# The first loads of a gated pair of linear-attention blocks: one queue in order of need, four chunks of x turned by TensorE

## The chip, the cores and the metric

The kernel runs on one core of a Trainium2 chip. The metric is the time of one execution on the device in microseconds (us), lower is better; a comparison takes the median of several runs. Traces are taken by the hardware profiler on one execution; times in them count from the span's start.

## The reference

Two linear-attention blocks A and B read the same `x` (2048 rows, 640 columns, bf16) and have their own weights. Their outputs are mixed by a gate computed per row from `x` and `gate_w`.

```python
def block(x, wqkv, wo):                      # 32 heads of 20
    q, k, v = split(x @ wqkv)                # each [head, 2048, 20]
    phi = lambda t: where(t > 0, t + 1, exp(t)) + 1e-6
    pq, pk = phi(q), phi(k)
    kv = einsum("bhsd,bhse->bhde", pk, v)
    z = einsum("bhsd->bhd", pk)
    num = einsum("bhqd,bhde->bhqe", pq, kv)
    den = einsum("bhqd,bhd->bhq", pq, z)[..., None] + 1e-6
    return merge_heads(num / den) @ wo

g = sigmoid((x * gate_w).sum(-1, keepdims=True))
out = g * block(x, A_wqkv, A_wo) + (1 - g) * block(x, B_wqkv, B_wo)
```

## The kernel before

All the matmuls need `x` twice: natural (`xn`, 16 chunks of 128 rows) and turned (`xT`, 640 columns on the partitions as 5 slices of 128, by 2048 rows). The k part of block A is made chunk by chunk: ten matmuls for a chunk of 128 rows (5 slices `c` times two halves `hf` of 320 columns), accumulated in a PSUM tile of two banks. The second half is one column wider (321): that column of `wkA` holds `gate_w`, so that the gate's logits fall out of the same matmul. `phi` then takes the PSUM tile through an exponential on ScalarE (ACT), and a `tensor_scalar` and a `scalar_tensor_tensor` on VectorE (DVE) into `pk`. The q part (`q_block`, `q_single`) multiplies slices of `wqA` with 512 rows of `xT`, and goes through the same `phi`. After k and q of A come the products G = x^T pk (partly by Strassen's scheme), normalisers, k and q of B, G of B, small products with `wv` and `wo`, and at the end the output products; nothing of that is touched by the change.

PSUM is used as four slots of two banks each (`ps(name, slot)`, tags ps0 to ps3); outside the hand-ordered parts `turn` hands them out in rotation, and after `k_first` it is set to 2.

The order at the start comes from the program for what lies in `tc.manual_schedule()`, which keeps each engine's instructions in the written order, and from the scheduler for what lies outside. Before the change, `k_first()` alone is in the first such scope; the first loads, the constants on GpSimd (POOL: `ident`, `I4`, `spread`, `I16`, `maskE`, `headE`), seven warm-up matmuls on constant ones, and the gate column (a transpose of the row `grow`, a copy on DVE to `gsb`, five copies on POOL into `wkA`) stand outside. After the scope, POOL clears `R` (L683) and copies `I16` into it four times (L688). `grow` lies in another part of `R`.

The first loads go over two queues. SP issues x0, `wkA` slices 0, 2 and 4, a transposing transfer of rows 256 to 511 (chunks 2 and 3) straight into `xT`, `wqA` in one piece, and three transposing transfers of 512 rows each. ACT issues the gate row, x1 and `wkA` slices 1 and 3. TensorE transposes x0 and x1 itself (`x_transpose`, L206) into PSUM, and DVE copies them into `xT` (L209). `k_first` interleaves chunks 0 and 1 over slices 0 to 2, finishes each with slices 3 and 4, and then does chunks 2 and 3 one after the other.

Of the kernel before, what the change touches and what calls it, by code (L numbers as in the profile page):

```python
# [8 lines left out]
P = 128  # L9
# [3 lines left out]
ALU = mybir.AluOpType  # L13

S, D, H = 2048, 640, 32
Dh = D // H
DT = D // P
ST = S // P
NB = 4
CB = 4  # L20
HB = 512
HF = D // 2
TW = 4
WB = (120, 120, 80)
# [7 lines left out]
def kernel(  # L32
# [11 lines left out]
    nc = tc.nc  # L44
# [13 lines left out]
    def ps_raw(name, slot=None):  # L58

        if slot is None:  # L60
            slot = turn[0]
            turn[0] = (slot + 1) % 4
        return psum.tile([P, 4 * HB], BF16, tag=f"ps{slot}", name=name)

    def ps(name, slot=None):

        return ps_raw(name, slot).bitcast(FP32).rearrange("p (b n) -> p b n", b=2)

    xT = persist.tile([P, DT, S], BF16, name="xT")
# [6 lines left out]
    ident = persist.tile([P, P], BF16, name="ident")  # L76
    I4 = persist.tile([P, H], BF16, name="I4")
    headE = persist.tile([P, H], BF16, name="headE")
    maskE = persist.tile([P, WB[0]], BF16, name="maskE")
    KVA = persist.tile([P, NW, WB[0]], BF16, name="KVA")  # L80
    spread = persist.tile([P, P], BF16, name="spread")
    R = persist.tile([P, 2, 4, RB], BF16, name="R")
    ones = persist.tile([P, H], BF16, name="ones")
    I16 = persist.tile([P, ST], BF16, name="I16")
# [18 lines left out]
    wq_dram = [A_wqkv.rearrange("(c p) f -> p c f", p=P), B_wqkv.rearrange("(c p) f -> p c f", p=P)]  # L103
# [5 lines left out]
    wk = [None, None]  # L109
    wv = [None, None]  # L110
    wq = [None, None]
    wk[0] = wpool.tile([P, DT, D + 16], BF16, tag="wk", name="wkA")
    def load_x(eng, i):
        eng.dma_start(out=xn[:, i, :], in_=x2[i * P:(i + 1) * P, :])

    def x_turned(lo, hi):
        nc.sync.dma_start_transpose(out=xT[:, :, lo:hi], in_=x2[lo:hi, :])

    def load_wk(eng, lo, hi):
        eng.dma_start(out=wk[0][:, lo:hi, 0:D], in_=wq_dram[0][:, lo:hi, D:2 * D])  # L120

    grow, logitT = R[0:DT, 0, 2, 0:P], R[:, 0, 1, 0:P]
    nc.scalar.dma_start(out=grow, in_=gate_w.rearrange("(c p) -> c p", p=P))
    load_x(nc.sync, 0)
    load_x(nc.scalar, 1)
    for c, eng in enumerate((nc.sync, nc.scalar, nc.sync, nc.scalar, nc.sync)):
        load_wk(eng, c, c + 1)
    x_turned(2 * P, HB)
    wq[0] = wpool.tile([P, DT, D], BF16, tag="wq", name="wqA")
    nc.sync.dma_start(out=wq[0][:], in_=wq_dram[0][:, :, 0:D])  # L130
    for n in range(1, NB):
        x_turned(n * HB, (n + 1) * HB)


    make_identity(nc, ident[:])
    for r in range(4):
        rows = slice(32 * r, 32 * r + 32)
        nc.gpsimd.tensor_copy(out=I4[rows], in_=ident[rows, rows])
    nc.gpsimd.tensor_copy(
        out=spread[:].rearrange("p (h t) -> p h t", t=TW), in_=I4[:, :, None].to_broadcast([P, H, TW])  # L140
    )
    nc.gpsimd.tensor_tensor(
        out=I16[0:2 * ST], in0=ident[0:2 * ST, 0:ST], in1=ident[0:2 * ST, ST:2 * ST], op=ALU.add
    )
    nc.gpsimd.memset(maskE[:], 1.0)
    for sign, base in ((1, 0), (-1, Dh - 1)):
        nc.gpsimd.affine_select(
            out=maskE[:], in_=maskE[:], pattern=[[-sign * Dh, WB[0] // Dh], [0, Dh]],
            compare_op=ALU.is_ge, fill=0.0, base=base, channel_multiplier=sign,
        )  # L150
    nc.gpsimd.memset(headE[:], 1.0)
    for sign, base in ((1, 0), (-1, TW - 1)):
        nc.gpsimd.affine_select(
            out=headE[:], in_=headE[:], pattern=[[-sign * TW, H]],
            compare_op=ALU.is_ge, fill=0.0, base=base, channel_multiplier=sign,
        )


    raw = ps_raw("warm", 3)
    warm = raw.bitcast(FP32).rearrange("p (b n) -> p b n", b=2)  # L160
    one_l, one_r = [nc.const_aps.tensor(1.0, [P, n], BF16) for n in (P, HB)]
    for k in range(7):
        nc.tensor.matmul(warm[:, 0, :], lhsT=one_l, rhs=one_r, start=True, stop=True)
    gcol = raw[:, 2 * HB:2 * HB + DT]
    nc.tensor.transpose(out=gcol, in_=grow, identity=ident[0:DT, 0:DT])
    gsb = work.tile([P, DT], BF16, tag="rT", name="gsb")
    nc.vector.tensor_copy(out=gsb[:], in_=gcol)
    for c in range(DT):
        nc.gpsimd.tensor_copy(out=wk[0][:, c, D:D + 1], in_=gsb[:, c:c + 1])

    def by_group(dst, lhsT, src, h):

# [28 lines left out]
    def gate_done(b):  # L201
        nc.vector.tensor_scalar(ge[b][:], ge[b][:], 1.0, 1e30, op0=ALU.add, op1=ALU.min)

    def x_transpose(i, pt, cuts=(0, DT)):
        for c in range(DT):
            nc.tensor.transpose(out=pt[:, c * P:(c + 1) * P], in_=xn[:, i, c * P:(c + 1) * P], identity=ident[:])  # L206
        src = pt[:, 0:D].rearrange("p (c n) -> p c n", c=DT)
        for lo, hi in zip(cuts, cuts[1:]):
            nc.vector.tensor_copy(out=xT[:, lo:hi, i * P:(i + 1) * P], in_=src[:, lo:hi])  # L209

    def phi(dst, src, n, lifted=False, side=None):

# [12 lines left out]
    def k_mm(b, i, c, pt, hf):  # L225
        w = HF + (hf if b == 0 else 0)
        nc.tensor.matmul(  # L227
            pt[:, hf, 0:w], lhsT=xT[:, c, i * P:(i + 1) * P], rhs=wk[b][:, c, hf * HF:hf * HF + w],
            start=(c == 0), stop=(c == DT - 1),
        )  # L230

    def k_done(b, i, pt):
        side = (lambda: nc.scalar.copy(out=logit[:, i:i + 1], in_=pt[:, 1, HF:HF + 1])) if b == 0 else None
        phi(pk[:, i, :].rearrange("p (b n) -> p b n", b=2), pt[:, :, 0:HF], HF, side=side)

    def k_chunk(b, i, slot=None):
        pt = ps(f"k{'AB'[b]}", slot)
        for hf in range(2):
            for c in range(DT):
                k_mm(b, i, c, pt, hf)  # L240
        k_done(b, i, pt)

    def k_first():

        pts = [ps("kA", 2 + i) for i in range(2)]
        raw = [ps_raw("xt", i) for i in range(2)]
        for i in range(2):
            x_transpose(i, raw[i], (0, 2, DT))

        def part(i, cs):  # L250
            for c in cs:
                for hf in range(2):
                    k_mm(0, i, c, pts[i], hf)

        for c in range(3):
            for i in range(2):
                part(i, (c,))
        for i in range(2):
            part(i, (3, 4))
            k_done(0, i, pts[i])  # L260
        for i in range(2, CB):
            k_chunk(0, i, i - 2)

    def mixed(t, m):

# [412 lines left out]


    with tc.manual_schedule():  # L680
        k_first()
    turn[0] = 2
    nc.gpsimd.memset(R[:, :, 0:2, :], 0.0)  # L683
    chosen = R[:, 1, 0:2, :].rearrange("p a (b n) -> p (a b) n", b=2)
    for h in range(2):
        for q in range(2):
            i0 = h * hc + q
            nc.gpsimd.tensor_copy(  # L688
                out=chosen[0:2 * ST, 2 * h + q, :].rearrange("p (j n) -> p j n", j=4),
                in_=I16[0:2 * ST, i0:i0 + hc - 1:2][:, :, None].to_broadcast([2 * ST, 4, 32]),  # L690
# [6 lines left out]
        q_single(0, DT - 1, n)  # L697
    for i in range(hc, ST - 2):
        k_chunk(0, i)
    for n in range(NB):  # L700
        lo, hi = max(n * CB, 2), (n + 1) * CB
        nc.sync.dma_start(
            out=xn[:, lo:hi, :], in_=x2[lo * P:hi * P, :].rearrange("(q p) d -> p q d", p=P)
        )
# [10 lines left out]
    with tc.manual_schedule():  # L715
# [21 lines left out]
        t = wpool.tile([P, 2, hc, HF], BF16, tag="wo", name="T13")  # L737
# [7 lines left out]
        t = wpool.tile([P, 2, DT, HF], BF16, tag="wq", name="TM12")  # L745
        TM[1], TM[2] = t[:, 0], t[:, 1]
        part = [slice(n * RB, (n + 1) * RB) for n in range(4)]
        half = ST // 2
# [64 lines left out]
        for i in range(half - 1):  # L813
            p, after = pairs[i:i + 2]
# [45 lines left out]
```

## Time and profile before

| | |
|---|---|
| median of 3 runs | 187.68 us (186.47 to 188.96) |
| profiled execution | 186.32 us |
| its span, first to last instruction | 184.6 us |
| TensorE (PE) busy | 180.5 us, 98% |
| VectorE (DVE) busy | 149.7 us, 81% |
| ScalarE (ACT) busy | 78.7 us, 43% |
| GpSimd (POOL) busy | 6.0 us, 3% |
| transfers, SP's queue | 16.72 MB, 32.8% of 16 engines' span |

The span is the part of the time that the trace shows; 1.7 us lie around it. A busy share is time with at least one instruction of that engine under way. The chain that ended last is followed back from the last instruction, at each step to what released it. Lines of a timeline give start, duration, engine, line of the program, operation, output and inputs, and how many instructions are merged.

### The profile page before, as it was taken

What the parts mean: (1) busy time and instruction counts of PE and PEld (TensorE: products, weight loads), DVE (VectorE), ACT (ScalarE), POOL (GpSimd) and SP (SyncE); (2) the same over time, 40 slices, a digit from 0 to 9 for tenths busy, and PEclk for the clock granted to TensorE, in tenths of its full rate; (3) what the DMA queues carried; (4) which work ended last, traced back from release to release, by engine and by line L of the source; (5) the groups of instructions that cost most, each with busy time, mean ns of one, the idle gap of its engine ahead of it and who ended that gap; (6) DMA issues with size and microseconds to landing.
All of it is one profiled execution on the core that took longest, in us unless ns stands there. A gap on an engine that the chain in (4) does not pass through costs nothing.

```text
span 184.6 us, 3375 instructions
## 1 busy us (share of the span) xinstructions
PE 180.5 (98%) x1338; PEld 121.2 (66%) x1338; DVE 149.7 (81%) x236; ACT 78.7 (43%) x132; POOL 6.0 (3%) x30
## 2 busy tenths in 40 slices
PE   7999999999999999999999999999999999999993
PEld 3656657755576677877775555566778777777772
DVE  1377869899998999799899998639689999877863
ACT  2345455557951501367674577531501763111010
POOL 7400000010000000000000000000000000000000
PEclk9999999999999999999999999999999999999999
DMA  5999999041140000011115000000524480023333
GB/s 163 306 215 186 280 376 248 10 132 47 11 170 0 0 4 0 0 35 35 55 34 190 15 0 0 0 4 0 178 70 112 145 214 1 36 107 110 108 107 108
DMA packets 21022, 17.59 MB, mean 95 GB/s; under 512 B 9998, under 2 KB 20750, under 8 KB 21006
## 3 DMA queue, kind: packets, MB, share of 16 engines
q1 hardware_dynamic: 20276, 16.72, 32.8%
q10 hardware_dynamic: 730, 0.66, 1.0%
q8 instruction: 10, 0.16, 0.4%
q14 instruction: 6, 0.05, 0.1%
HBM read 10.81 MB, written 4.26 MB: 82 GB/s over the span
## 4 chain that ended last, share of the span: by engine, by line
PE 95%; DMA 2%; ACTq 1%; DVE 0%; issue 0%
PE gs L351 17%; PE ox L575 12%; PE kB L227 12%; PE qB L274 12%; PE kA L227 12%; PE qA L274 6%; PE oz L575 6%; PE qA L285 5%; PE gB L324 2%; PE gA L324 2%; PE ow L575 2%; DMA wkA<-in_A_wqkv_dram 2%; PE qA L295 1%; PE s L476 1%; PE mA L476 1%; PE kvA L446 1%
## 5 line engine op out<-in xcount | busy, mean ns | idle before, releaser
L227 PEld LDWEIGHTS <-xT 128*128 128x128 bf16 x320 | 31.1, 98 | 12.8 <-DVE xT L209 0.4
L219 DVE TENSOR_SCALAR e<-e 128x640 bf16<-128x640 bf16 (+2 forms) x53 | 18.9, 357 | 8.7 <-ACT e L214 8.1
L227 PE MATMUL kB<-wkB,xT 128*128 128x320 bf16 x160 | 23.0, 299 | 0.0
L227 PE MATMUL kA<-wkA,xT 128*128 128x320 bf16 (+1 forms) x160 | 22.6, 300 | 0.2
L274 PE MATMUL qB<-xT,wqB 128*128 128x512 bf16 x100 | 21.8, 379 | 0.0
L214 ACT ACTIVATE e<-kB 128x640 bf16<-128x640 f32 x16 | 11.3, 704 | 18.8 <-PE kB L227 17.5
L274 PEld LDWEIGHTS <-wqB 128*128 128x128 bf16 x100 | 11.7, 117 | 9.8 <-issue 0.2
L214 ACT ACTIVATE e<-kA 128x640 bf16<-128x640 f32 x16 | 11.2, 705 | 12.3 <-PE kA L227 12.3
L223 DVE SCALAR_TENSOR_TENSOR pk<-kA,e 128x640 bf16<-128x640 f32 x16 | 13.2, 825 | 2.1 <-DVE e L219 0.2
L223 DVE SCALAR_TENSOR_TENSOR pk<-kB,e 128x640 bf16<-128x640 f32 x16 | 13.2, 825 | 1.7
L214 ACT ACTIVATE e<-qB 128x1024 bf16<-128x1024 f32 x10 | 10.2, 1024 | 8.7 <-PE qB L274 8.3
L214 ACT ACTIVATE e<-qA 128x1024 bf16<-128x1024 f32 (+1 forms) x11 | 10.4, 947 | 8.2 <-PE qA L285 5.1
L625 ACT COPY u<-ox 128x320 f32<-128x320 f32 x8 | 3.4, 426 | 20.4 <-PE ox L575 20.4
L351 PEld LDWEIGHTS <-S 128*128 128x128 bf16 x96 | 9.4, 98 | 3.6
L351 PEld LDWEIGHTS <-xn 128*128 128x128 bf16 x96 | 9.1, 98 | 4.0 <-issue 0.4
L274 PE MATMUL qA<-xT,wqA 128*128 128x512 bf16 x50 | 11.0, 379 | 0.0
L575 PEld LDWEIGHTS <-xT 128*128 128x128 bf16 x85 | 8.1, 98 | 2.9
L575 PEld LDWEIGHTS <-pqTB 128*128 128x128 bf16 x80 | 7.8, 98 | 3.2
L575 PEld LDWEIGHTS <-pqTA 128*128 128x128 bf16 x80 | 7.8, 98 | 2.9
L351 PE MATMUL gs<-pk,xn 128*128 128x320 bf16 x64 | 9.4, 300 | 0.0
L223 DVE SCALAR_TENSOR_TENSOR pqTB<-qB,e 128x1024 bf16<-128x1024 f32 x7 | 8.6, 1225 | 0.7
L274 PEld LDWEIGHTS <-wqA 128*128 128x128 bf16 x50 | 5.9, 117 | 4.8
(138 smaller groups left out, 286.5 us busy)
## 6 DMA issues: line engine op xcount, KB each, us to landing
out_dram<-pk SPq DMA_DIRECT2D x14, 160.0 KB, 1.8
xn<-in_A_x_dram SPq DMA_DIRECT2D x3, 640.0 KB, 5.7
wqA<-in_A_wqkv_dram SPq DMA_DIRECT2D x1, 800.0 KB, 6.0
wvA<-in_A_wqkv_dram SPq DMA_DIRECT2D x1, 800.0 KB, 9.7
wkB<-in_B_wqkv_dram SPq DMA_DIRECT2D x1, 800.0 KB, 4.7
wqB<-in_B_wqkv_dram SPq DMA_DIRECT2D x1, 800.0 KB, 4.7
MA<-mA_dram SPq DMA_DIRECT2D x1, 800.0 KB, 4.6
wvB<-in_B_wqkv_dram SPq DMA_DIRECT2D x1, 800.0 KB, 4.6
```

The source lines that it names most:

```text
L214: nc.scalar.activation(out=e[:], in_=src, func=ACT.Exp)
L219: nc.vector.tensor_scalar(e[:], e[:], 1.0, EPS, op0=ALU.min, op1=ALU.add)
L223: nc.vector.scalar_tensor_tensor(out=dst, in0=src, scalar=1.0 + EPS, in1=e[:], op0=ALU.add, op1=ALU.max)
L227: nc.tensor.matmul(pt[:, hf, 0:w], lhsT=xT[:, c, i * P:(i + 1) * P], rhs=wk[b][:, c, hf * HF:hf * HF + w], start=(c == 0), stop=(c == DT - 1),
L274: nc.tensor.matmul(pt[:, u, :], lhsT=mixed(wq[b][:, c, :], m), rhs=xT[:, c, n * HB:(n + 1) * HB], start=(c == 0), stop=(c == DT - 1),)
L285: nc.tensor.matmul(pt[:, u, :], lhsT=mixed(wq[b][:, c, :], m + u), rhs=xT[:, c, n * HB:(n + 1) * HB], start=(c == 0), stop=(c == DT - 1),)
L295: nc.tensor.matmul(pt[:, 0, :], lhsT=mixed(wq[b][:, c, :], m), rhs=xT[:, c, n * HB:(n + 1) * HB], start=(c == 0), stop=(c == DT - 1),)
L324: nc.tensor.matmul(pt[:, hf, 0:HF], lhsT=xn[:, i, c * P:(c + 1) * P], rhs=pk[:, i, hf * HF:(hf + 1) * HF], start=(i == 0), stop=(i == ST - 1),
L351: nc.tensor.matmul(pt[:, n, 0:HF], lhsT=left[:, i, n * P:(n + 1) * P], rhs=right[:, i, :], start=(first and i == 0), stop=(i == hc - 1), s ...
L476: nc.tensor.matmul(dst[:w, 0:HF], lhsT=KVA[:w, k, 0:w], rhs=wo_sb[b][:w, k, n * HF:(n + 1) * HF], start=True, stop=True,)
L575: nc.tensor.matmul(dst, lhsT=left[:, c, r0:r0 + P], rhs=right[:, c, :], start=(first and c == 0), stop=(c == DT - 1), skip_group_check=not ...
L625: nc.scalar.copy(out=self.u6[:], in_=self.at("x"))
```

## The change

- The first loads become a function, `first_loads`, called first in the hand-ordered scope. All of them but the gate row go over SP's queue, in this order: x0, x1, x2, x3, `wkA` slices 0, 1, 2, and 3 with 4, `wqA` slices 0 and 1, `wqA` slices 2 to 4, then the three transposing transfers of rows 512 to 2047. The transposing transfer of rows 256 to 511 is gone.
- The constants become a function, `constants`, called second in the same scope.
- The warm-ups are five of 512 columns and two of 128. They, the gate column and the transposes are now part of `k_first`.
- TensorE transposes all four first chunks, and DVE copies each in two pieces; the gate column comes between those of chunk 0.
- The k matmuls of the four chunks are interleaved: slices 0 and 1 in a written order, slice 2 of all, then slices 3 and 4 with `phi` chunk by chunk. Chunks 2 and 3 use PSUM slots 0 and 1, in which the transposes were.
- The natural load of `xn` after the q part leaves out the first four chunks, which are there.

```diff
-    nc.scalar.dma_start(out=grow, in_=gate_w.rearrange("(c p) -> c p", p=P))
-    load_x(nc.sync, 0)
-    load_x(nc.scalar, 1)
-    for c, eng in enumerate((nc.sync, nc.scalar, nc.sync, nc.scalar, nc.sync)):
-        load_wk(eng, c, c + 1)
-    x_turned(2 * P, HB)
     wq[0] = wpool.tile([P, DT, D], BF16, tag="wq", name="wqA")
-    nc.sync.dma_start(out=wq[0][:], in_=wq_dram[0][:, :, 0:D])
-    for n in range(1, NB):
-        x_turned(n * HB, (n + 1) * HB)
+
+    def first_loads():
+
+        nc.scalar.dma_start(out=grow, in_=gate_w.rearrange("(c p) -> c p", p=P))
+        for i in range(CB):
+            load_x(nc.sync, i)
+        for lo, hi in ((0, 1), (1, 2), (2, 3), (3, DT)):
+            load_wk(nc.sync, lo, hi)
+        for lo, hi in ((0, 2), (2, DT)):
+            nc.sync.dma_start(out=wq[0][:, lo:hi, :], in_=wq_dram[0][:, lo:hi, 0:D])
+        for n in range(1, NB):
+            x_turned(n * HB, (n + 1) * HB)
+
+    def constants():
+
...
-    for k in range(7):
-        nc.tensor.matmul(warm[:, 0, :], lhsT=one_l, rhs=one_r, start=True, stop=True)
     gcol = raw[:, 2 * HB:2 * HB + DT]
-    nc.tensor.transpose(out=gcol, in_=grow, identity=ident[0:DT, 0:DT])
+
+    def warm_up(n, w):
+        for k in range(n):
+            nc.tensor.matmul(warm[:, 0, 0:w], lhsT=one_l, rhs=one_r[:, 0:w], start=True, stop=True)
+
     gsb = work.tile([P, DT], BF16, tag="rT", name="gsb")
-    nc.vector.tensor_copy(out=gsb[:], in_=gcol)
-    for c in range(DT):
-        nc.gpsimd.tensor_copy(out=wk[0][:, c, D:D + 1], in_=gsb[:, c:c + 1])
+
+    def gate_column():
+        nc.tensor.transpose(out=gcol, in_=grow, identity=ident[0:DT, 0:DT])
+
+    def gate_copy():
+        nc.vector.tensor_copy(out=gsb[:], in_=gcol)
+        for c in range(DT):
+            nc.gpsimd.tensor_copy(out=wk[0][:, c, D:D + 1], in_=gsb[:, c:c + 1])
...
-        for i in range(2):
-            x_transpose(i, raw[i], (0, 2, DT))
+        half = [raw[i % 2][:, i // 2 * 2 * HB:] for i in range(CB)]
...
-        for c in range(3):
-            for i in range(2):
-                part(i, (c,))
-        for i in range(2):
+        warm_up(5, HB)
+        warm_up(2, P)
+        x_transpose(0, half[0])
+        gate_column()
+        x_copy(0, half[0], 0, 2)
+        gate_copy()
+        x_copy(0, half[0], 2, DT)
+        for i in range(1, CB):
+            x_transpose(i, half[i])
+            for lo, hi in ((0, 2), (2, DT)):
+                x_copy(i, half[i], lo, hi)
+        pts += [ps("kA", i) for i in range(2)]
+        for i, c in ((0, 0), (1, 0), (2, 0), (0, 1), (1, 1), (3, 0), (2, 1), (3, 1)):
+            part(i, (c,))
+        for i in range(CB):
+            part(i, (2,))
+        for i in range(CB):
             part(i, (3, 4))
             k_done(0, i, pts[i])
-        for i in range(2, CB):
-            k_chunk(0, i, i - 2)
...
     with tc.manual_schedule():
+        first_loads()
+        constants()
         k_first()
...
-    for n in range(NB):
-        lo, hi = max(n * CB, 2), (n + 1) * CB
+    for n in range(1, NB):
+        lo, hi = n * CB, (n + 1) * CB
```

The body of `constants` is unchanged but for its indentation.

More of the change, by code (lines that the diff above doesn't have):

```diff
@@ L135 @@
[L135 to L149, printed above, removed]
-        )
@@ L151 @@
[L151 to L155, printed above, removed]
-        )
+    wq[0] = wpool.tile([P, DT, D], BF16, tag="wq", name="wqA")
+    def first_loads():
[8 more added lines that the diff above has]
+            x_turned(n * HB, (n + 1) * HB)
@@ new lines, in constants @@
+    def constants():
+        make_identity(nc, ident[:])
+        for r in range(4):
+            rows = slice(32 * r, 32 * r + 32)
+            nc.gpsimd.tensor_copy(out=I4[rows], in_=ident[rows, rows])
+        nc.gpsimd.tensor_copy(
+            out=spread[:].rearrange("p (h t) -> p h t", t=TW), in_=I4[:, :, None].to_broadcast([P, H, TW])
+        )
+        nc.gpsimd.tensor_tensor(
+            out=I16[0:2 * ST], in0=ident[0:2 * ST, 0:ST], in1=ident[0:2 * ST, ST:2 * ST], op=ALU.add
+        )
+        nc.gpsimd.memset(maskE[:], 1.0)
+        for sign, base in ((1, 0), (-1, Dh - 1)):
+            nc.gpsimd.affine_select(
+                out=maskE[:], in_=maskE[:], pattern=[[-sign * Dh, WB[0] // Dh], [0, Dh]],
+                compare_op=ALU.is_ge, fill=0.0, base=base, channel_multiplier=sign,
+            )
+        nc.gpsimd.memset(headE[:], 1.0)
+        for sign, base in ((1, 0), (-1, TW - 1)):
+            nc.gpsimd.affine_select(
+                out=headE[:], in_=headE[:], pattern=[[-sign * TW, H]],
+                compare_op=ALU.is_ge, fill=0.0, base=base, channel_multiplier=sign,
+            )
@@ L202, in gate_done, with x_transpose, x_copy @@
         nc.vector.tensor_scalar(ge[b][:], ge[b][:], 1.0, 1e30, op0=ALU.add, op1=ALU.min)
-    def x_transpose(i, pt, cuts=(0, DT)):
+    def x_transpose(i, pt):
         for c in range(DT):
             nc.tensor.transpose(out=pt[:, c * P:(c + 1) * P], in_=xn[:, i, c * P:(c + 1) * P], identity=ident[:])
+    def x_copy(i, pt, lo, hi):
         src = pt[:, 0:D].rearrange("p (c n) -> p c n", c=DT)
-        for lo, hi in zip(cuts, cuts[1:]):
-            nc.vector.tensor_copy(out=xT[:, lo:hi, i * P:(i + 1) * P], in_=src[:, lo:hi])
+        nc.vector.tensor_copy(out=xT[:, lo:hi, i * P:(i + 1) * P], in_=src[:, lo:hi])
     def phi(dst, src, n, lifted=False, side=None):
```

## The prediction

> **What bounds the kernel now.** I read the page's busy shares and slices first, then the chain that ended last in order of time, then the timeline of the first 20 us.
>
> ```profile
> PE 180.5 (98%) x1338; PEld 121.2 (66%) x1338; DVE 149.7 (81%) x236; ACT 78.7 (43%) x132; POOL 6.0 (3%) x30
> ...
> PE   7999999999999999999999999999999999999993
> ```
>
> TensorE is full in every slice but the first and the last. So there is nothing to win after the start, and whatever delays the first dense matmuls is handed on to the end undiminished. The chain says when they begin (start us, us, what):
>
> ```profile
> 1.80 3.97 DMA wkA<-in_A_wqkv_dram
> 5.77 0.04 issue
> 5.81 5.07 PE kA L227 x36
> 10.88 4.36 PE qA L285 x20
> 15.24 1.08 PE qA L295 x5
> 16.32 5.45 PE kA L227 x40
> ```
>
> The start is set by the second slice of wkA (on ACT's queue), which lands at 5.77. Only 4 of the 40 k matmuls of the first four chunks run ahead of it; 36 follow without a gap, then the q blocks, then k chunk 4. Forty k matmuls take 5.45, 0.136 each. The timeline has the pieces that the change moves (start, us, engine, line):
>
> ```profile
> 0.84 2.97 PE L163 MATMUL warm<-const-bfloat16-1.0 128*128 128x512 bf16 x7 [0.84 <-PEq L844]
> ...
> 3.62 0.20 POOL L153 TENSOR_SCALAR_AFFINE_SELECT headE<-headE 128x32 bf16<-128x32 bf16 x1
> ...
> 3.85 0.45 PE L206 MATMUL xt<-ident,xn 128*128 128x128 bf16 x5
> ...
> 4.19 0.66 POOL L169 COPY wkA<-gsb 128x1 bf16<-128x1 bf16 x5 [0.37 <-DVE gsb L167]
> 4.35 1.18 DVE L209 COPY xT<-xt 128x256 bf16<-128x256 bf16 x4 [0.22 <-PE xt L206]
> ...
> 4.78 0.95 POOL L683 MEMSET R<- 128x1024 bf16 x1
> ...
> 5.79 0.98 POOL L688 COPY R<-I 32x128 bf16<-32x128 bf16 x4
> ...
> 7.64 0.70 ACT L214 ACTIVATE e<-kA 128x640 bf16<-128x640 f32 x1 [3.60 <-PE kA L227]
> ...
> 8.86 0.82 DVE L223 SCALAR_TENSOR_TENSOR pk<-kA,e 128x640 bf16<-128x640 f32 x1 [0.15 <-DVE e L219]
> ...
> 10.72 4.51 PE L285 MATMUL qA<-xT,wqA 128*128 128x512 bf16 x20
> ```
>
> The reader is to see three things. POOL finishes its constants at 3.82, then writes the gate column into wkA (4.19 to 4.85), and only afterwards touches R (memset 0.95, four copies 0.98). phi of a k chunk ends 2.04 after its exp starts (7.64 to 9.68). And chunk 0's phi is over at 9.68, a microsecond before TensorE wants that PSUM slot for q at 10.72.
>
> **The change, part by part.** *Loads.* SP now issues x0 to x3, wk 0, 1, 2, 3-4, wq 0-1, wq 2-4, and then three transposing transfers; ACT keeps the gate row. An issue takes SP about 0.46 (x0 at 0.81, the first wk slice at 1.26), so the fifth, wk 0, goes out near 2.7 where it went at 1.26. x0 landed 2.3 after its issue, at 3.1. The slices behind it follow at the rate of the transfers:
>
> ```profile
> 2.00:3.00 1.00, 1.00 (x4) 0.36 (x3) 0.00 (x0) 0.24 (x1) 0.79 (x5) 1.00 0.90 228
> ...
> 4.00:5.00 1.00, 0.83 (x12) 0.53 (x10) 0.71 (x4) 0.04 (x1) 0.81 (x6) 1.00 0.97 344
> ...
> 8.00:9.00 1.00, 1.00 (x10) 0.73 (x8) 0.47 (x2) 1.00 (x4) 0.00 (x0) 1.00 1.04 364
> ```
>
> The last column of these stretches is GB/s: 228 while the first bytes of SP's queue ran almost alone, 344 with both queues, 364 with SP's alone again. A 160 KB slice (0.164 MB) takes 0.48 at 344 and 0.72 at 228. So wk 0 lands at 3.1 + 4 x 0.48 = 5.0 (6.0 at 228), wk 1 at 5.5 (6.7), wk 2 at 6.0 (7.4), wk 3-4 at 6.9 (8.9), wq 0-1 at 7.9 (10.3), the rest of wq at 9.3 (12.5). I take 344, since SP's queue reached 364 alone.
>
> *TensorE's front.* Five warm-ups of 0.43 (2.97 / 7 = 0.424) and two of about 0.11 end near 3.2, when x0 is there. Four groups of five transposes (0.45 each as recorded) replace two. In the instruction order of the changed kernel, chunk 2's transposes wait for DVE's copies of chunk 0 and chunk 3's for those of chunk 1. A pair of copies takes 0.62 (1.18 for two pairs), gsb 0.16: chunk 0's copies run about 3.9 to 4.7, chunk 1's to 5.35, chunk 3's transposes 5.4 to 5.85. All k matmuls are behind them.
>
> *POOL.* Here the order matters most. The constants now stand inside the hand-made order, and in the changed kernel's instruction stream the R memset comes second on POOL, the four R copies stand among the mask operations, and the gate column comes last. The work ahead of it is everything that POOL did before: constants 3.28 (sum of their durations from 0.80), R memset 0.95, R copies 0.98: 5.21. Before, 3.28 of durations fitted into 3.02, 0.92 of their sum, since starts overlap. So 0.80 + 0.92 x 5.21 = 5.6 (6.0 without overlap, 5.3 if overlap is better), plus 0.19 for the first of the five copies and 0.04 to be seen: 5.83. The second matmul, which has the gate column (321 wide), waits for it; behind it stand all k matmuls. Ident, needed by the transposes, slips by the memset from 1.53 to about 2.2, still ahead of x0.
>
> Three legs therefore end together: wk 0 at 5.0 to 6.0, transposes at 5.85, gate column at 5.83. One matmul runs ahead; 39 follow from 5.83: next free at 5.83 + 39 x 0.136 = 11.1. Later wk slices are wanted at 6.5, 7.9 and 9.0, after they land. Before, this point was 10.72: **+0.4**.
>
> *The q wait.* The new loop finishes all four chunks at the end: chunk 0's last matmul is the 28th, with only 12 behind it (12 x 0.136 = 1.63). It starts at 5.83 + 26 x 0.136 = 9.37, takes 0.30 (mean of the group), exp starts at 9.70, phi ends 2.04 later at 11.74, seen at 11.8. The first q block uses that PSUM slot (turn 2) and its matmul waits on DVE: 11.8 instead of 11.1, **+0.7**. That cover was a full microsecond before. Later slots are free in time: DVE releases one k chunk every 1.19 (8.86 to 10.05), so 12.9, 14.1, 15.3, while TensorE wants them at 14.0, 16.1 and 17.2.
>
> *Costed at nothing.* The transposing transfers are issued near 5.8 instead of 5.33, but the one of 256 rows is gone; the first used to land 8.4 after issue, at 13.8, and k chunk 4 wants it at 16.3 then and 17.3 now. If that cover went, each late microsecond would count. Ten more transposes and four more DVE copies lie before 5.85, in time that was waiting. ACT loses three issues; its table load moves forward, harmless. One of four late x loads shrinks out of SP's queue at 18; x is read there only at the first G pass near 49.
>
> **Sum.** q starts at 11.8 instead of 10.72: +1.1. The profiled execution took 186.32, span 184.6 and 1.7 around it; the same execution would be 187.4. The median of the runs is 187.68, 1.36 above the profiled one; on that base the change gives 187.68 + 1.1 = **188.8**, +0.6%, under the 2% that a measurement of this kernel can about tell from no change.
>
> **Rivals.** *B, one queue is slow.* At 228 GB/s it costs 0.2 at wk 0 and wk 1 and as much at the rest of wq (12.5 where the third q matmul wants it at 12.2). At 200 (0.82 a slice) the rest of wq, the 13th slice behind x0, lands at 13.8, and q's third matmul, formerly at 11.15, moves by 2.6: 190.3. For it: the 228 row. Against: 364 on the same queue, at larger pieces.
>
> *C, the clock is released late.* Seven warm-ups ran at 0.424 for 512 columns, the later q matmuls at 0.218 (4.36 / 20 = 0.218): half speed, until about 3.4 to 3.9, some 2.8 after the first matmul, although the granted-clock column shows 1.00 throughout. Now dense matmuls stop at 3.2, and until 5.83 there are only short groups of transposes. If the release needs another 2.8 of dense matmuls from there, it comes at 8.6, and 2.8 at half speed loses 1.4: 187.68 + 1.1 + 1.4 = 190.2. Against: 2.4 of dense work are there before the pause, and the transposes at 3.85 already ran fast. The Trainium skill (TensorE: Matmul & The Clock Gate, Part 1 and Part 4) says that the release goes by free-running windows of 3.4 us and that transposes don't count as busy; by that rule two warm-ups fewer make the release depend on where the window lies, which is rival C in part of the executions. One profile of before can't show that.
>
> *D, not slower.* The start of before varies between executions: the runs reach from 186.47 to 188.96. If in ordinary runs wk 1 on ACT's queue lands later than in the profile, by the 1.36 between profile and median, before starts at 7.2, while the new order is set by POOL at 5.83 and not by that slice. Then the change ends at 187.4 and before at 187.68: equal or better, from the point where wk 1 lands later than 5.77 + 1.1 = 6.9. For it: it heads the chain. Against: nothing shows that the scatter lies there. That POOL is faster can't do it alone: with wk 0 at 5.0 and everything else ready, q still starts at 5.0 + 6.0 = 11.0, +0.3.
>
> **Chances.** Forecast 0.52, B 0.12, C 0.18, D 0.18. The range takes D's 187.4 with half of the scatter between runs below it, and B's and C's 190.3 with a little above: 186.8 to 191.0. Faster by over 2% would need -3.7, which no case has: 0.01. Slower by over 2% needs +3.8, B and C together: 0.06. The rest, 0.93, is within 2%.
>
> **What would show it.** Right: the gate column's copies on POOL at 5.5 to 6.0 and the second k matmul just behind; q's first matmul at 11.6 to 12.0, released by DVE's phi of chunk 0; from there everything shifted by 1.1, span 185.7. Wrong: k matmuls dense before 5.3, q's first matmul released by a transfer of wq (B), k matmuls spaced 0.27 after 5.8 (C), or k chunk 4 waiting for its transposing transfer.

## The result, and the profile after

The changed kernel takes 187.83 us (median of 22 runs) where the kernel before takes 186.81 (22 runs): +1.0 us, 0.55%. The recorded ratio is 1.0067, 95% interval 1.0039 to 1.0094; a second comparison, on another occasion, gave 1.0040 (1.0015 to 1.0066). So it is slower, by about half a per cent, and within 2%. The span of the profiled execution goes from 184.6 to 186.1, +1.5. Executions of either kernel do not all agree: most lie within 0.7 us of the fastest, the others up to 3.2 us above it, and the ratio leaves out what is more than 1.5% above the fastest of its kernel (two of the kernel before, none of the changed one). What may set the late ones apart is taken up under the clock, below.

The page's busy shares and slices of the changed kernel:

```profile
PE 180.9 (97%) x1343; PEld 122.4 (66%) x1348; DVE 150.1 (81%) x240; ACT 78.5 (42%) x132; POOL 6.0 (3%) x30
...
PE   8889999999999999999999999999999999999993
```

TensorE is as busy as it was, in a longer span, and besides the last the thin slices are now the first three. The chain that ended last, cut to the first 20 us (start us, us, what):

```profile
5.25 0.45 PE xt L216 x5
5.71 0.03 issue
5.73 0.45 PE xt L216 x5
6.18 3.94 PE kA L238 x28
10.13 0.02 issue
10.15 0.71 ACT e L225
...
10.89 0.34 DVE e L230
...
11.37 0.84 DVE pk L234
12.20 0.04 issue
12.24 0.38 PE qA L306
...
16.72 1.08 PE qA L316 x5
17.80 2.31 PE kA L238 x17
```

Before, this stretch was 36 k matmuls and then q at 10.72, TensorE alone. Now the chain goes through TensorE only for 28 k matmuls, leaves it for ACT and DVE (phi of chunk 0), and comes back at q's first matmul, at 12.24: 1.5 later. k chunk 4 begins 1.5 later too (17.8 for 16.3), and so does everything behind it. The timeline of the same piece:

```profile
3.93 0.71 PE L216 MATMUL xt<-ident,xn 128*128 128x128 bf16 x5
...
5.25 0.28 PEld L216 LDWEIGHTS <-xn 128*128 128x128 bf16 x5 [0.87 <-DMA xn<-in_A_x_dram]
...
5.71 0.65 POOL L179 COPY wkA<-gsb 128x1 bf16<-128x1 bf16 x5
5.73 0.28 PEld L216 LDWEIGHTS <-xn 128*128 128x128 bf16 x5 [0.20 <-DMA xn<-in_A_x_dram]
...
6.14 5.61 PE L238 MATMUL kA<-wkA,xT 128*128 128x320 bf16 x40
...
12.24 4.48 PE L306 MATMUL qA<-xT,wqA 128*128 128x512 bf16 x19 [0.49 <-DVE pk L234]
```

The weight loads of the transposes (PEld) wait for x2 until 5.25 and for x3 until 5.73; the gate column is written from 5.71; k starts at 6.14. In the trace the pieces land one after the other on the one queue: x0 at 3.06, x1 at 3.53, x2 at 5.21, x3 at 5.69, wk 0 at 6.10, wk 1 at 6.51, wk 2 at 7.96, wk 3-4 at 9.18, the rest of wq at 12.35. The chain shows no wait of k for wk 0, because the ends of matmuls are modelled and the transposes' reach 6.18. But the last transpose started at 5.96, and before the change k's first matmul started 0.06 after the last transpose: here it was wk 0, at 6.10, that let k start.

### The profile page after: what moved, and what is told of

Read it like the earlier page. It is cut to its first block, busy times and chain, and to the rows that moved or that the text cites. A ratio compares the mean times of both kernels' runs of the same rounds, so it can differ in the third digit from the quotient of the medians.

```text
span 186.1 us, 3393 instructions
## 1 busy us (share of the span) xinstructions
PE 180.9 (97%) x1343; PEld 122.4 (66%) x1348; DVE 150.1 (81%) x240; ACT 78.5 (42%) x132; POOL 6.0 (3%) x30
## 4 chain that ended last, share of the span: by engine, by line
PE 96%; DVE 1%; issue 1%; ACT 0%; DVEq 0%
PE gs L372 17%; PE ox L596 12%; PE kB L238 12%; PE qB L295 12%; PE kA L238 11%; PE qA L295 6%; PE oz L596 5%; PE qA L306 5%; PE gB L345 2%; PE gA L345 2%; PE ow L596 2%; PE warm L169 1%; PE qA L316 1%; PE xt L216 1%; PE s L497 1%; PE mA L497 1%
## 5 line engine op out<-in xcount | busy, mean ns | idle before, releaser
L295 PEld LDWEIGHTS <-wqB 128*128 128x128 bf16 x100 | 11.7, 117 | 9.8 <-issue 0.2
L295 PE MATMUL qA<-xT,wqA 128*128 128x512 bf16 x49 | 10.9, 379 | 0.1
L306 PE MATMUL qA<-xT,wqA 128*128 128x512 bf16 x38 | 8.8, 379 | 0.6 <-DVE pk L234 0.5
```

Of the source, the lines that this page charges most:

```text
L295: nc.tensor.matmul(pt[:, u, :], lhsT=mixed(wq[b][:, c, :], m), rhs=xT[:, c, n * HB:(n + 1) * HB], start=(c == 0), stop=(c == DT - 1),)
L306: nc.tensor.matmul(pt[:, u, :], lhsT=mixed(wq[b][:, c, :], m + u), rhs=xT[:, c, n * HB:(n + 1) * HB], start=(c == 0), stop=(c == DT - 1),)
```

## Experiments

**What holds the start: POOL or the loads?** Three kernels take one leg away each, or both. The first puts only `ident` ahead of the gate column on POOL; the clearing of `R` and the four copies into it move behind with the other constants.

```diff
     def constants():
-        make_identity(nc, ident[:])
...
         first_loads()
-        constants()
+        make_identity(nc, ident[:])
         k_first()
+        constants()
+        nc.gpsimd.memset(R[:, :, 0:2, :], 0.0)
...
```

> Changed kernel with POOL's order mended: only ident stands ahead of the gate column, the other constants and the clearing of R behind it. Theory (two legs end almost together: the slices on SP's one queue, wk 0 landing at 6.10, and POOL's gate column at 5.89; then a wait of 0.65 for phi of chunk 0): the gate column is written at 4.3 to 5.0, but the first k matmul stays at 6.1 because wk 0 lands then; q's first matmul stays at 12.2 to 12.3, ratio to the kernel before 1.007 as for the changed kernel. Rival (POOL alone held the start): dense k matmuls at 5.6 to 5.7, q at 11.8, ratio 1.004.

Its timeline:

```profile
4.39 0.67 POOL L178 COPY wkA<-gsb 128x1 bf16<-128x1 bf16 x5 [3.01 <-DVE gsb L176]
...
6.19 5.61 PE L237 MATMUL kA<-wkA,xT 128*128 128x320 bf16 x40 [0.41 <-DMA wkA<-in_A_wqkv_dram]
...
12.29 4.48 PE L305 MATMUL qA<-xT,wqA 128*128 128x512 bf16 x19 [0.49 <-DVE pk L233]
```

The gate column is there 1.3 earlier and nothing moves: k starts at 6.19, and the wait beside it names wkA's transfer. The rival falls: POOL's order did not hold this execution. The ratio, 1.0043 (1.0022 to 1.0063), doesn't tell the two theories apart by itself; the timeline does.

The second spreads the natural loads over two queues, with POOL's order as in the change; the third does both.

```diff
         for i in range(CB):
-            load_x(nc.sync, i)
-        for lo, hi in ((0, 1), (1, 2), (2, 3), (3, DT)):
-            load_wk(nc.sync, lo, hi)
+            load_x((nc.sync, nc.scalar)[i % 2], i)
+        for k, (lo, hi) in enumerate(((0, 1), (1, 2), (2, 3), (3, DT))):
+            load_wk((nc.sync, nc.scalar)[k % 2], lo, hi)
```

> Changed kernel with its natural loads over two queues: x0, x2, wk 0, wk 2 on SP, x1, x3, wk 1, wk 3-4 on ACT. Theory: x2, x3 and wk 0 land 0.5 to 0.9 earlier, and the gate column on POOL (5.89) becomes the last leg; dense k matmuls from 5.9, q's first matmul at 12.0, ratio to the kernel before 1.005 to 1.006. Rival (the one queue alone held the start): dense from 5.3 to 5.4, q at 11.5, ratio 1.003.

> Changed kernel with both edits: two queues and POOL's order mended. Theory: neither leg is left; the next is TensorE's transposes of chunk 3, which wait for DVE's copies of chunk 1 (end about 5.4): dense k matmuls from 5.5 to 5.7, q's first matmul at 11.6 to 11.8, more than the two edits give one by one; ratio 1.003 to 1.005. A rest of about +0.9 over the kernel before stays, since the wait for phi is not touched.

Both came out at 1.0132 (1.0077 to 1.0186, and 1.0083 to 1.0181): slower than the change (1.0067 and 1.0040), where each theory had them faster. Two queues bring x1 later, not earlier: it is issued behind the gate row and lands at 4.71 in both, where the single queue has it at 3.53, and TensorE pauses before chunk 1's transposes. That alone doesn't explain a per cent. Groups of matmuls of the second kernel (two queues) by shape, in the stretch from 7.0 to 9.5, with the mean ns of one:

```profile
L238 PE MATMUL kA<-wkA,xT 128*128 128x320 bf16 x5 | 2.4, 473 | 0.0
L238 PE MATMUL kA<-wkA,xT 128*128 128x321 bf16 x4 | 1.9, 475 | 0.0
```

And the same stretch of the changed kernel:

```profile
L238 PE MATMUL kA<-wkA,xT 128*128 128x321 bf16 x10 | 2.8, 300 | 0.0
L238 PE MATMUL kA<-wkA,xT 128*128 128x320 bf16 x10 | 2.8, 299 | 0.0
```

Nine matmuls against twenty in the same 2.5 us: TensorE still runs at half speed there, until 9.8 in this trace. This is the prediction's rival C, met in another kernel. What the two queues would give with the clock up is therefore only seen in part: in the third kernel's profiled execution, which is the fastest of its six, k starts at 6.13 although the gate column is done at 5.1 and wk 0 has landed at 5.25; chunk 3's transposes, at 5.85, are what is left. The seventh k matmul then waits for wk 1, which lands at 7.16 on ACT's queue, and q comes at 12.49, no earlier than with one queue (12.24).

**Is the wait for phi real?** Chunks 0 and 1 are finished before slice 2 of chunks 2 and 3 begins; the rest is the change.

```diff
-        for i in range(CB):
-            part(i, (2,))
-        for i in range(CB):
-            part(i, (3, 4))
-            k_done(0, i, pts[i])
+        for j in (0, 2):
+            for i in (j, j + 1):
+                part(i, (2,))
+            for i in (j, j + 1):
+                part(i, (3, 4))
+                k_done(0, i, pts[i])
```

> Changed kernel with chunks 0 and 1 finished before slice 2 of chunks 2 and 3 is begun: chunk 0's last k matmul is the 24th instead of the 28th. Theory: 16 matmuls (2.2) instead of 12 (1.6) lie behind it, which covers phi; but wk 3-4 (landing up to 9.2) is now wanted at 8.9, which costs about 0.3: q's first matmul at 12.0 instead of 12.25, ratio to the kernel before 1.005. Rival (the wait for phi is not what holds q, the transfer of wq at 12.35 is): q stays at 12.3 or later, ratio 1.007 to 1.009.

```profile
6.08 5.70 PE L238 MATMUL kA<-wkA,xT 128*128 128x320 bf16 x40 [0.26 <-DMA wkA<-in_A_wqkv_dram]
...
10.85 0.83 DVE L234 SCALAR_TENSOR_TENSOR pk<-kA,e 128x640 bf16<-128x640 f32 x1
...
11.72 0.38 PE L307 MATMUL qA<-xT,wqA 128*128 128x512 bf16 x1
```

k starts where it did (6.08 for 6.14), phi of chunk 0 ends half a microsecond earlier (10.85 + 0.83 = 11.68 for 12.21), and q's first matmul follows at 11.72 for 12.24. So the wait was real, and reordering takes 0.5 of it back; 0.1 is left, since k alone would have let q start at 11.62. The feared 0.3 for wk 3-4 did not come, by luck: it landed at 8.84, 0.05 before it was wanted, where the change's own trace has it at 9.18. The span is 185.6, also 0.5 less; the ratio, 1.0035 (1.0011 to 1.0059), lies on the expected side but overlaps that of the change.

**The clock.** First the warm-ups of the change alone, in the kernel before:

```diff
-    for k in range(7):
-        nc.tensor.matmul(warm[:, 0, :], lhsT=one_l, rhs=one_r, start=True, stop=True)
+    for n, w in ((5, HB), (2, P)):
+        for k in range(n):
+            nc.tensor.matmul(warm[:, 0, 0:w], lhsT=one_l, rhs=one_r[:, 0:w], start=True, stop=True)
```

> Kernel before, with five warm-ups of 512 columns and two of 128 instead of seven of 512. Theory: transposes of x0 start at 3.2 instead of 3.85, but wk 1 still sets k's dense start at 5.8: nothing gained, median ratio 0.999 to 1.003; the pause before dense matmuls grows, so more executions have the late clock, 1 to 2.5 us above the median (before: 4 of 22). Rival (the number of warm-ups is without effect on the clock): the same share of late executions and ratio 1.000.

The ratio is 1.0020 (0.9986 to 1.0055), median 187.73 against 186.99; 5 of its 12 executions are above 188, where 3 of 25 of the kernel before beside it were, too few to count as shown. In the profiled execution k starts early, at 5.37, but at half speed for more than three microseconds (stretch 5.3 to 8.5, by shape), and q comes at 12.48 instead of 10.72:

```profile
L228 PE MATMUL kA<-wkA,xT 128*128 128x321 bf16 x6 | 2.9, 475 | 0.0
L228 PE MATMUL kA<-wkA,xT 128*128 128x320 bf16 x6 | 2.8, 469 | 0.0
```

Then the changed kernel with still fewer:

```diff
-        warm_up(5, HB)
+        warm_up(2, HB)
```

> The changed kernel with two warm-ups of 512 columns instead of five (and the two of 128). Theory (dense matmuls before 6 decide when the clock is released): transposes of chunk 0 still wait for x0 at 3.1, dense k matmuls start at 6.1 to 6.2 as before, but at 0.27 each for 2 to 3 us in all or nearly all executions; q's first matmul at 13.3 to 14, ratio to the kernel before 1.012 to 1.018. Rival (warm-ups do nothing that the transposes don't do): ratio 1.007, k matmuls at 0.136 from the first.

The ratio is 1.0141 (1.0114 to 1.0169), as the theory had it, against 1.0040 for the change on the same occasion; even its profiled execution, the fastest of the six at 187.99, starts k slowly (5.9 to 6.6):

```profile
L238 PE MATMUL kA<-wkA,xT 128*128 128x320 bf16 x2 | 0.9, 469 | 0.0
...
L238 PE MATMUL kA<-wkA,xT 128*128 128x321 bf16 x1 | 0.5, 475 | 0.0
```

Its q came at 12.45, so the forecast of 13.3 to 14 missed this execution; the slower ones have no trace. The reverse, more warm-ups, went into a kernel that also has POOL's order mended and chunks 0 and 1 finished early:

```diff
         for i in range(1, CB):
             x_transpose(i, half[i])
+            warm_up((0, 2, 1, 0)[i], HB)
```

> Changed kernel with POOL's order mended, chunks 0 and 1 finished early, and three more warm-ups of 512 columns in TensorE's pauses between the transposes (two behind chunk 1's, one behind chunk 2's). Theory (in part of the executions the clock is released late because too few dense matmuls run before 6): k dense from 6.2, q's first matmul at 11.7 as with the early finish alone, median ratio to the kernel before 1.003 to 1.005, and no execution more than 1 us above the median, where the changed kernel had 6 of 22. Rival (the late executions come from somewhere else): the same median, and again about a quarter of the executions 1.5 to 2 us above it.

Its 12 executions lie between 187.25 and 188.01, ratio 1.0023 (1.0003 to 1.0043). Its trace:

```profile
5.29 0.74 PE L215 MATMUL xt<-ident,xn 128*128 128x128 bf16 x5
...
6.12 0.44 PE L215 MATMUL xt<-ident,xn 128*128 128x128 bf16 x5
...
6.40 5.61 PE L237 MATMUL kA<-wkA,xT 128*128 128x320 bf16 x40
...
11.96 4.48 PE L307 MATMUL qA<-xT,wqA 128*128 128x512 bf16 x19
```

No execution was late, as the theory had it, but nothing shows that the warm-ups did it. In the trace they did not bring the clock up earlier: chunk 2's transposes still ran slowly at 5.29 (0.74) and chunk 3's fast at 6.12 (0.44), and the extra warm-ups, run at half speed, moved k to 6.40 and q to 11.96, where 6.2 and 11.7 were expected. The kernel with only POOL's order mended, without extra warm-ups, had no execution above 188.07 in 12 either. And the control failed:

> The changed kernel once more, beside the next one on the same chip. Theory (part of the executions release the clock late): ratio near 1.007, most executions at 187.5 to 188.1 and up to a quarter 1.5 to 2 us above these. If no execution lies there, the late clock belongs to the chip or the hour as much as to the kernel.

This time no execution of the changed kernel lay above 188.70, in 12, where it had been 6 of 22 above 189.1. How often an execution is late thus differs from one occasion to the next, by more than these few runs can attribute to three extra warm-ups. That the late ones are late by the clock is not shown: none of the changed kernel's six has a trace. The granted clock cannot decide it, since it reads 0.998 to 1.000 for them and 1.000 for the kernel with two queues too, which ran at half speed until 9.8. In the kernel before, the six that took over 189 us in the later comparisons read 0.991, so these may be late for another reason. In this second trace of the changed kernel the loads were a little quicker: wk 0 landed at 5.88, k began at 5.92 and q at 12.02.

**Can the start of the kernel before be made earlier?** Three attempts, the last in two versions, none faster. One queue alone:

```diff
-    load_x(nc.scalar, 1)
-    for c, eng in enumerate((nc.sync, nc.scalar, nc.sync, nc.scalar, nc.sync)):
+    load_x(nc.sync, 1)
+    for c, eng in enumerate((nc.sync,) * 5):
```

> Kernel before, with x1 and all five wk slices on SP's queue and nothing else changed. Theory (the single queue itself costs little; what costs is that x2 and x3 go ahead of wk): the third piece, wk 0, lands at 4.8 to 5.2 and wk 1 at 5.3 to 5.7; k dense from 5.3 to 5.7, at or a little before 5.81; ratio 0.998 to 1.001. Rival (one queue is slower than two): wk 1 lands after 6.2, k dense from 6.2 or later, ratio 1.002 to 1.005.

```profile
4.10 2.42 SPq L117 DMA_TRANSPOSE xT<-in_A_x_dram  x1
...
5.10 3.36 PE L227 MATMUL kA<-wkA,xT 128*128 128x320 bf16 x20
...
6.57 0.58 SPq L130 DMA_DIRECT2D wqA<-in_A_wqkv_dram  x1
...
13.18 1.06 PE L285 MATMUL qA<-xT,wqA 128*128 128x512 bf16 x3 [1.54 <-DMA wqA<-in_A_wqkv_dram]
```

The theory is right about the front (x1 at 3.64, wk 0 at 4.47, k without a pause from 5.57, where the kernel before has 5.81, until it waits for wk 4, which lands at 7.45) and wrong about the result, 1.0072 (1.0046 to 1.0098). wk 0 is third on its one queue here and fifth in the change, where it lands 1.6 later: what holds k in the change is x2 and x3 ahead of wk 0, more than the single queue. Three more issues stand ahead of the transposing transfer on SP (4.10 for 2.68), wqA goes out at 6.57 for 4.70 and lands at 13.14, and q waits for it. The change avoids just this, by having no transposing transfer ahead of wq.

The gate row third on ACT's queue:

```diff
-    nc.scalar.dma_start(out=grow, in_=gate_w.rearrange("(c p) -> c p", p=P))
     load_x(nc.sync, 0)
...
         load_wk(eng, c, c + 1)
+        if c == 1:
+            nc.scalar.dma_start(out=grow, in_=gate_w.rearrange("(c p) -> c p", p=P))
```

> Kernel before, with the gate row third on ACT's queue instead of first, so that x1 and wk 1 are issued 0.55 earlier. Theory: wk 1 lands near 5.2 to 5.4 instead of 5.77 and x1 near 3.9; k dense from 5.3, q's first matmul at 10.3, unless wqA (10.68) then holds it: ratio 0.997 to 1.000. Rival (the bytes are served at a fixed rate, whatever their order): wk 1 still near 5.7, no change.

Ratio 1.0085 (1.0053 to 1.0116). x1 lands at 3.93 and wk 1 at 4.82, earlier than hoped, but the gate row lands only at 4.64, and TensorE's transpose of it stands ahead of x0's in program order:

```profile
4.69 0.18 PE L166 MATMUL warm<-ident,R 5*128 5x5 bf16 x1 [0.70 <-DMA R<-in_gate_w_dram]
...
5.91 7.57 PE L228 MATMUL kA<-wkA,xT 128*128 128x320 bf16 x40
```

TensorE pauses 0.70 before 4.69, although x0 landed at 3.75. All seven warm-ups have run, but the k matmuls follow each other at 0.267 until about 9.8 and at 0.136 after it: the 40 take 7.57 where the kernel before takes 6.11 from its first to its last.

At last the slices exchanged between the queues and wqA behind them on ACT's, with seven warm-ups and with eight:

```diff
-    load_x(nc.scalar, 1)
-    for c, eng in enumerate((nc.sync, nc.scalar, nc.sync, nc.scalar, nc.sync)):
+    load_x(nc.sync, 1)
+    for c, eng in enumerate((nc.scalar, nc.sync, nc.scalar, nc.sync, nc.scalar)):
...
-    nc.sync.dma_start(out=wq[0][:], in_=wq_dram[0][:, :, 0:D])
+    nc.scalar.dma_start(out=wq[0][:], in_=wq_dram[0][:, :, 0:D])
```

> Kernel before with x1 behind x0 on SP's queue, the wk slices 0, 2, 4 on ACT's and 1, 3 on SP's, and wqA on ACT's queue behind them, so that SP still issues four loads ahead of its first transposing transfer. Theory (the start is set by x1 and the wk slices, then by wqA): x1 lands at 3.6, wk 1 at 5.0 to 5.4, wqA at 9 to 10; k dense from 5.0 to 5.4, q's first matmul at 10.0 to 10.4, ratio 0.996 to 0.999, faster than the kernel before. Rival (the transfers share one rate and only change places): wk 1 or wk 2 near 5.8, wqA near 10.7, ratio 1.000.

> The kernel of b4_swap with eight warm-ups of 512 columns instead of seven. Theory: transposes start near 4.2 instead of 3.85, k dense still from 5.0 to 5.5, q at 10.0 to 10.5; fewer executions with the late clock, so a narrower spread; median ratio 0.996 to 0.999. Rival: the longer warm-up delays chunk 1's copies and with them k, 0.3 more than b4_swap.

Both are the slowest of all: 1.0192 (1.0142 to 1.0243) and 1.0184 (1.0145 to 1.0222). In the first, x1 landed at 4.72 (3.6 expected), wk 1 at 6.07 and wqA at 11.51, and k chunk 2 waits for its transposing transfer:

```profile
12.33 2.90 PE L227 MATMUL kA<-wkA,xT 128*128 128x320 bf16 x20 [3.88 <-DMA xT<-in_A_x_dram]
```

That transfer of 256 rows was issued at 3.08 and landed at 12.28, 9.2 after, while wqA moved on the other queue; in the kernel before it was issued at 2.68 and landed at 7.73. In the second kernel wk 1 landed only at 7.43, for which k waited 1.27, and the transfer at 11.88.

## Why the prediction was right, and where it was off

The forecast was 188.8 for a median of 187.68, +1.1; measured are +1.0 between the medians and +1.5 between the profiled spans. q's first matmul came at 12.24, a little behind the 11.6 to 12.0 that were to show the forecast right (12.02 in the second execution), and it was released by DVE's phi of chunk 0, as forecast. Against the median of before over 22 runs, 186.81, the forecast's +1.1 gives 187.9, and 187.83 was measured; the level of 188.8 was too high because the first three runs of before had a median 0.9 higher. That +1.1 fits +1.0 so well is in part luck. The sum was worked out on the profiled execution of before, and between the profiled executions it is 0.4 short. But the median of before lies 0.5 above its profiled execution (186.81 for 186.32), and that of the change does not (187.83 for 187.79), which takes about as much off again.

*The wait for phi, +0.7: right.* Its place, its cause (PSUM slot of chunk 0, 12 matmuls of cover) and its size hold: k alone would have let q start at 6.14 + 5.45 = 11.59, it started at 12.24, 0.65 later. Finishing chunk 0 four matmuls earlier removed 0.5.

*The later end of k, +0.4: right in kind, mis-sized.* Measured, it is 11.59 - 10.72 = 0.9 in the profiled execution, and 5.92 + 5.45 - 10.72 = 0.65 in the second one. The term that failed is the price of a slice on SP's queue: I took 0.48 (344 GB/s), so wk 0 at 5.0. From x0 (3.06) to wk 0 (6.10) four pieces took 3.04, 0.76 each; 0.71 in the second execution. The transposes went by the same step: chunk 3's waited for x3 until 5.73, not for DVE's copies of chunk 1, which ended at 5.24. These are the stretches of the changed kernel, GB/s in the last column:

```profile
3.00:4.00 1.00, 1.00 (x10) 0.77 (x9) 0.08 (x1) 0.00 (x0) 0.92 (x5) 1.00 1.01 234
4.00:5.00 1.00, 0.64 (x5) 0.38 (x5) 0.86 (x5) 0.00 (x0) 1.00 (x6) 1.00 0.75 202
5.00:6.00 1.00, 0.72 (x10) 0.56 (x11) 0.49 (x3) 0.00 (x0) 1.00 (x7) 1.00 1.00 307
```

The bound made from the queue's first stretch in the kernel before (228), wk 0 at 6.0, is what came, but not by its reasoning. From 2.0 to 6.0 the changed kernel moved 257 on average (287 in the stretch ahead of those shown), 1.03 MB, while the five pieces up to wk 0 are 0.82 MB. So part of the pieces behind wk 0 had moved before it landed, and the rate of the queue alone would have put it at 5.6. The 364 that I leaned on belongs to a later stretch with an 800 KB transfer in it. So a part of rival B is in the result, at its lower price; its higher one, q waiting for the rest of wq, stayed away: that landed at 12.35 and the third q matmul ran at 12.68.

*POOL's order, "here the order matters most": the place was right, the weight wrong.* The column was written from 5.71 (5.6 forecast), but moving it to 4.39 changed nothing, since wk 0 lands at 6.1. It is not the last leg. In the second execution of the changed kernel, with wk 0 at 5.88, the two fall together within 0.1.

*Rival C is a real mechanism, though neither trace of the change shows its cost.* In the profiled execution of the change the second group of transposes still took 0.71 and the third 0.45, so the clock came up between 4.4 and 5.3, later than before (by 3.85) and just ahead of k; in the second execution it was up by 3.93. The Trainium skill (TensorE: Matmul & The Clock Gate, Part 1) says that the window is 3.4 us long and runs free, so that the moment varies from run to run. These traces agree that it varies, with full speed from 3.85, from 3.93, from about 5 and from 9.8; the length of the window none of them shows. One trace speaks against the rival's other premise, that transposes do not count: in the kernel with two warm-ups nothing but transposes ran from 2.1 to 5.9, and the clock came up at about 6.7, after 0.8 of k matmuls. That fewer warm-ups cost time is shown by that kernel (1.0141 against 1.0040); how much of the +1.0 between the medians comes from the warm-ups that the change shortens is not settled: the changed kernel with all seven was not run, and in the kernel before they cost 0.2%, with an interval that includes nothing.

*Rival D fell away.* The change is slower, not equal. D lived on the 1.36 between the profiled execution and the median of before; over 22 runs the median lies only 0.5 above the profiled 186.32.

*What was costed at nothing* stayed so: the transposing transfers were issued from 5.6, the first landed at 15.5, and k chunk 4 began at 17.8 without waiting for it.

## What to carry to other kernels

When TensorE is full after the start, read the start as a set of legs, and price a load by the stretch in which the same queue was last seen doing the same thing, not by its best stretch; and keep in mind that a piece can land later than the rate of its queue says, when pieces behind it move too. Before interleaving chunks so that they all finish at the end, count the matmuls that are left behind the first one's last: they have to cover the whole chain that frees its PSUM slot (here 2.07 from the end of its matmuls, against 12 x 0.136 = 1.63). Pauses ahead of the first dense matmuls are not free even where a load would have ended them anyway, because the clock may come up later (at about 9.8 with two queues and with the gate row third).

## What was not expected of the hardware

- A transposing transfer of 256 rows took 9.2 from issue to landing beside an 800 KB load on the other queue (8.8 in the kernel with eight warm-ups), and 5.0 when that load stood behind it on the same queue.
- Five 160 KB pieces on one queue do not land at an even pace: after x1 there is a hole of 1.7 in the profiled execution of the change (x2 at 5.21), of 1.0 with POOL's order mended (3.78 to 4.80), and in the second execution of 1.1, one piece later (x2 at 4.16, x3 at 5.28). No run here shows why.
- k matmuls of 320 and 321 columns followed each other at 0.267 instead of 0.136 for 2.7 us (7.1 to 9.8) in the kernel with two queues, after pauses of TensorE that lasted less than a microsecond each, and from 5.9 to 9.8 with the gate row third, after seven warm-ups and one pause of 0.70.
